# A Strassen level for a weight product, four differences on GpSimd, and two moves in the order of the work

## The chip, the cores and the metric

The kernel runs on one core of a Trainium2 chip. A core has a matrix engine (TensorE, PE in the profile), a vector engine (VectorE, DVE), an activation engine (ScalarE, ACT), a general engine (GpSimd, POOL), a queue engine that issues transfers (SyncE, SP), and DMA engines that move data. Each engine works through its own list of instructions in order and waits on semaphores for the others. The metric is the time of one execution on the device in microseconds (us). Before the change it is 325.35 us (median of 3 runs, 325.21 to 325.37).

## The reference

Inputs are q, k, v of shape (8 batches, 8 heads, 1024 positions, 64), E and F of shape (64, 1024), and weights w1, w2 (512 x 1024) and w_out (1024 x 512). Attention is over a projected sequence of length 64, and its output is the input of a maxout layer:

```python
k_proj = einsum('ks,bhsd->bhkd', E, k)
v_proj = einsum('ks,bhsd->bhkd', F, v)
attn   = softmax(q @ k_proj^T / sqrt(64))          # over the 64 projected positions
x      = (attn @ v_proj) as (8192 tokens, 512)
g      = maximum(x @ w1, x @ w2)
out    = g @ w_out                                 # (8192, 512), float32
```

## The kernel before, in words

The kernel writes the maximum as `x @ w2 + relu(x @ (w1 - w2))`. So `out = x @ M + relu(x @ wd) @ w_out` with `M = w2 @ w_out` (512 x 512) and `wd = w1 - w2`. It makes `wd_sb` on VectorE (`step_wd`, L430), `w2` transposed on TensorE (`step_w2t`, L436) and `m_sb`, which is M, on TensorE (`step_m`, L450) once, near the start, and then goes over the batches.

**Tiles.** A batch has 1024 tokens. The work after attention is cut into 16 units of 512 tokens, two to a batch: unit 0 and 1 are batch 0, unit 2 and 3 are batch 1, and so on. A unit has an "up" half (x @ wd and the relu, `up_steps`, L552) and a "down" half (the sum with M and w_out, `down_steps`, L623). Batch 0's up half is done plainly (`up_slots`, L407, eight blocks for each half of the batch); all other halves are one level of Strassen: a 2 x 2 block product with seven block products instead of eight. The seven are called p1, p2, p6, p5, p7, p3, p4 and come in this order. They share two PSUM banks in turn (X, Y, X, Z, X, Z, X, where Z is Y's bank again). After each product the bank is copied to SBUF by `keep` (L540, tile `p_sb`), or added to what was kept and written to its goal by VectorE. The next product in that bank cannot start before this.

**Sums and differences.** Strassen needs sums of blocks of the left factor and differences of blocks of the right one. `step_s` (L524, instructions on L532) makes the first: `sums_x` of x, `sums_g` of g. `sub4` (L480, instructions on L488) makes the second: `step_t(0)` from w_out, `step_t(1)` from M (both into `T_sb`, for the down half) and `step_tw` from wd (four tiles of 128 x 1024 fp16 in `big0`, used by the up halves from unit 2 on). All of these run on VectorE. In `sub4` the second difference reads the first and the fourth reads the second.

**The order of the work is written by hand.** The pool is in manual schedule, so each engine's list follows the order of the program. `slots` is a list of TensorE steps with keys: `(0, n)` for the start (n = 10 to 15 are batch 0's last up blocks and n = 16 to 19 the four row blocks of M), `("P", n, p, i)` for piece i of product p of unit n's down half, `("U", n, h, i)` for a product of the up half of unit n + 1, and `("G", n, h)` for a group of attention. `at_slot(key, step)` hangs other steps behind a slot. Unit 0's down half has 14 pieces of six matmuls; between them the attention of batch 1 is placed by a list of names (L850 to L871): `kv` (projection of k and v, L188, whose end frees a buffer and lets the loads of batch 2's v and q be issued), `kpt` and `qt` (transposes), `sc` (scores), `dn` and `in` (denominators), `at` (values). From unit 1 on, the attention of the next batch is done in groups (`step_group`, L346) between the pieces.

**Queues.** Loads of q, k, v and of the weights convert float32 to fp16 and are issued by GpSimd. Stores of the result are issued by SyncE, as are the transposing DMAs that make q^T (`step_qt_dma`, L257) from batch 2 on, in two halves of four heads. One queue is one list: a DMA that waits holds back those behind it. Batch 2's q^T is used by the group `("G", 1, 1)` (first half) and `("G", 2, 0)` (second half). The result tiles `o_sb` come from `opool` with 4 buffers. A copy of one element on GpSimd (`step_gate`, L237, tile `junk`) waits for q^T so that later loads do not start earlier.

Of the kernel before, what the change touches and what calls it, by code (L numbers as in the profile page):

```python
# [9 lines left out]
FP16 = mybir.dt.float16  # L10
LN_EXP_SET = 6
ACTF = mybir.ActivationFunctionType
ALU = mybir.AluOpType
# [3 lines left out]
def kernel(  # L17
# [12 lines left out]
    nc = tc.nc  # L30

    B, H, S, D = q.shape
# [5 lines left out]
    NFB = DF // 128  # L38
    NDC = DM // 128
    NP2 = H // 2  # L40
    HALF = S // 2
# [8 lines left out]
    stage = ctx.enter_context(tc.tile_pool(name="stage", bufs=4))  # L50
    xpool = ctx.enter_context(tc.tile_pool(name="xpool", bufs=2))
    gpool = ctx.enter_context(tc.tile_pool(name="gpool", bufs=2))
    opool = ctx.enter_context(tc.tile_pool(name="opool", bufs=4))
    ppool = ctx.enter_context(tc.tile_pool(name="ppool", bufs=4))
    ps = ctx.enter_context(tc.tile_pool(name="ps", bufs=1, space=bass.MemoryType.PSUM))

# [1 line left out]
    turn = [0, 1, 2, 3]  # L58

    def mm_bank(dtype=FP32, n=None):  # L60
        if n is None:
            n = turn.pop(0)
            turn.append(n)
        return ps.tile([128, 512 if dtype == FP32 else 1024], dtype, tag=f"mm{n}", name="mm_ps")

    def att_banks(dtype=FP32):
# [9 lines left out]
            name=nc.get_next_instruction_name(),  # L76
# [82 lines left out]
    for i in range(2):  # L159
        eft_ps = mm_bank()  # L160
        for c in range(NC):
            nc.tensor.transpose(
                out=eft_ps[:, c * KP : (c + 1) * KP],
                in_=ef_v[:, i, c, :],
# [3 lines left out]
        eng = nc.scalar.copy if i else nc.vector.tensor_copy  # L168
# [97 lines left out]
    Z = D // 2  # L266
# [135 lines left out]
    wd_sb = const.tile([128, NDC, DF], FP16)  # L402
    m_sb = const.tile([128, NDC, DM], FP16)
    w2t_sb = big(3).rearrange("p (f m) -> p f m", f=NFB)
# [42 lines left out]
            out=w2t_sb[:, fb : fb + 2, :].rearrange("q f m -> q (f m)"), in_=ps_t  # L447
        )

    def step_m(r):  # L450
        m_ps = mm_bank(n=(1, 2, 0, 3)[r])
        for fb in range(NFB):
            nc.tensor.matmul(  # L453
                out=m_ps, lhsT=w2t_sb[:, fb, r * 128 : (r + 1) * 128], rhs=wo_sb[:, fb, :],
                start=(fb == 0), stop=(fb == NFB - 1),
            )
        nc.scalar.copy(out=m_sb[:, r, :], in_=m_ps)

# [6 lines left out]
    NG = NFB // 2  # L465
    NX = NDC // 2
    CH = DM // 2
    units = [(b, o) for b in range(B) for o in range(2)]
    U = {(b, o): {"n": n, "b": b, "o": o, "t": tiles[b]} for n, (b, o) in enumerate(units)}

    T_sb = const.tile([128, 4, NG + NX, CH], FP16)


    box = {}
# [2 lines left out]
        for i in which:  # L477
            box[i] = big(i)

    def sub4(T, blk, which=range(4)):  # L480
        for i in which:
            out_, x, y = (
                (T[0], blk(0, 1), blk(0, 0)),
                (T[1], blk(1, 1), T[0]),
                (T[2], blk(1, 1), blk(0, 1)),
                (T[3], blk(1, 0), T[1]),
            )[i]
            nc.vector.tensor_tensor(out=out_, in0=x, in1=y, op=ALU.subtract)  # L488

    def step_t(part, which=range(4)):  # L490
        n0, n1, src = ((0, NG, wo_sb), (NG, NG + NX, m_sb))[part]
        hs = n1 - n0
        sub4(
            [T_sb[:, i, n0:n1, :] for i in range(4)],
            lambda h, c: src[:, h * hs : (h + 1) * hs, c * CH : (c + 1) * CH], which,
        )

    def s_g(i):
        return box[2].rearrange("q (s n m) -> q s n m", s=4, n=NG)[:, i]
# [9 lines left out]
    def step_tw(i):  # L509
        sub4(  # L510
            [t_w(i) for i in range(4)],
            lambda h, c: wd_sb[:, h * NX : (h + 1) * NX, c * HALF : (c + 1) * HALF], (i,),
        )

    def x_blk(u, j, h):
# [5 lines left out]
        return u["gt"][:, h * NG : (h + 1) * NG, j * W : (j + 1) * W]  # L521


    def step_s(u, blk, S, which):  # L524
        for i in which:
            x, y, op = (
                (blk(u, 1, 0), blk(u, 1, 1), ALU.add),
                (S(0), blk(u, 0, 0), ALU.subtract),
                (blk(u, 0, 0), blk(u, 1, 0), ALU.subtract),
                (blk(u, 0, 1), S(1), ALU.subtract),  # L530
            )[i]
            nc.vector.tensor_tensor(out=S(i), in0=x, in1=y, op=op)  # L532

    def sums_x(u, which):
        step_s(u, x_blk, lambda i: s_x(i, u), which)
# [197 lines left out]
    t = tiles[0]  # L733
# [35 lines left out]
    u0, u1 = [*up_slots(t, 0)], [*up_slots(t, 1)]  # L769
# [12 lines left out]
    def loads(b, *names):  # L782
# [20 lines left out]
        (None, wd[2]), (None, wt[1]), (6, u1[2]), (7, u1[3]), (None, wt[2]), (None, wt[3]), (8, u0[4]), (9, u0[5]), (None, wd[3]),  # L803
        (10, u1[4]), (11, u1[5]), (12, u0[6]), (13, u0[7]),
        (14, u1[6]), (15, u1[7]),
        *((16 + n, lambda n=n: step_m(n)) for n in range(NDC)),
    ]
    slots = [((0, n), x) for n, x in slots]

# [24 lines left out]
    def at_slot(key, s, *a):  # L834
        steps.setdefault(key, []).append(lambda: s(*a))


    for key, s_, *a in (
        (10, open_box, 1), (11, sums_x, U[0, 0], (2,)), (12, sums_x, U[0, 0], (0,)),
        (13, sums_x, U[0, 0], (1,)), (14, sums_x, U[0, 0], (3,)), (15, open_box, 0, 2),  # L840
        (15, sums_g, U[0, 0], (0, 1)), (16, step_t, 0), (16, sums_g, U[0, 0], (2, 3)),
        *((17 + i // 3, step_tw, i) for i in range(4)), (19, open_box, 3),
    ):
        at_slot((0, key), s_, *a)


    t = tiles[1]
    at_slot((0, 19), new_attn, t)
    at_slot((0, 19), lambda: turn.__setitem__(slice(None), [2, 3]))
    for n, x in enumerate((  # L850
        "", "", "kv", "", "kpt", "qt00 qt10", "", "sc00 sc10", "qt01", "qt11", "",
        "dn00 in00 dn10 in10", "", "", "at00 AT10 sc01",
    )):
        key = ("P", 0, (n - 1) // 2, (n - 1) % 2) if n else (0, 19)
        for name in x.split():
            if name[0] == "k":
                if name == "kpt":
                    at_slot(key, step_kpt, t, 0, H, True)
                else:
                    at_slot(key, step_kv, t, 0, H, "kv", True)  # L860
                    at_slot(key, loads, 2, "v", "q")
            else:
                g, j = int(name[2]), int(name[3])
                s_ = {"qt": step_qt, "sc": step_sc,
                      "dn": step_dn, "in": step_inv, "at": step_at, "AT": step_at}[name[:2]]
                args = (4 * g, 4, 2 * j, 2 * j + 2) if name[:2] == "qt" else (g, j)
                at_slot(key, s_, t, *args, *([True] if name[:2] == "AT" else []))
        if n in (1, 5):
            at_slot(key, step_t, 1, (0, 1) if n == 1 else (2, 3))
        if 6 <= n < 10:  # L870
            at_slot(key, sums_x, U[0, 1], ((2, 0, 1, 3)[n - 6],))  # L871
# [11 lines left out]
    for b in range(3, B):  # L883
        t = tiles[b]
        n = 2 * b - 3
# [74 lines left out]
```

The softmax here doesn't subtract the row's maximum and nothing guards it: scores larger than these inputs give would overflow.

## Time and profile before

| | before |
|---|---|
| time, median of 3 runs | 325.35 us (325.21 to 325.37) |
| span of the profiled execution | 324.9 us, TensorE clock 1.00 |
| TensorE matmul busy | 316.1 us, 97% |
| VectorE busy | 236.6 us, 73%, 420 instructions |
| ScalarE busy | 203.2 us, 63% |
| GpSimd busy | 40.4 us, 12%, 60 instructions |
| moved by DMA | 53.14 MB, 164 GB/s on average |

Busy time is the time in which an engine had an instruction in work. For TensorE the ends are modelled, so a share of 97% says that it rarely stood idle, not that it was at its peak. A group of instructions is shown with its line, engine, operation, output and inputs, count, busy time and the mean duration of one, and then how long the engine stood idle before it and who ended that wait. In a timeline a line is: start, duration, engine, line, operation, with the idle time before in brackets. The window of interest here is the first 90 us, where all that the diff touches lies.

### The profile page before, as it was taken

Reading aid. Unit: us, or ns where it says so; the run is one execution under the profiler, and the core shown is the slowest. Engines: PE = TensorE matmul, PEld = TensorE weight load, DVE = VectorE, ACT = ScalarE, POOL = GpSimd, SP = SyncE. Lnnn points to the kernel's source line nnn. Section 1 sums busy time; section 2 is a strip of 40 time slices with the busy share of each in tenths; the row PEclk is TensorE's granted clock in tenths of the full one; section 3 lists DMA queues with packets and bytes.
Section 4 is the critical chain, followed back from the end, with each engine's and each line's share of the span. In section 5 each row is a group of like instructions: output and inputs, shape, how many; then the busy total and the mean of one; then the engine's idle time right before and its main releaser. Section 6 shows DMA issues by size and latency. Waiting matters only on the chain.

```text
span 324.9 us, 9012 instructions
## 1 busy us (share of the span) xinstructions
PE 316.1 (97%) x3852; PEld 248.5 (76%) x3852; DVE 236.6 (73%) x420; ACT 203.2 (63%) x364; POOL 40.4 (12%) x60
## 2 busy tenths in 40 slices
PE   7989999999999999999999999999999999999995
PEld 3555457877887888878887888868887888888884
DVE  1365797895968787877967786986967796969572
ACT  2366522566776777667776777656776777764541
POOL 8559002003000300021000300030000000000000
PEclk9999999999999999999999999999999999999999
DMA  7999999999999899599969899489959230312133
GB/s 154 206 199 184 205 204 206 217 205 177 204 232 224 140 195 245 149 168 165 228 131 196 152 208 235 131 163 185 228 113 215 51 100 32 99 34 98 34 119 109
DMA packets 76280, 53.14 MB, mean 164 GB/s; under 512 B 29520, under 2 KB 76112, under 8 KB 76240
## 3 DMA queue, kind: packets, MB, share of 16 engines
q0 software_dynamic: 30976, 28.31, 55.3%
q1 hardware_dynamic: 45264, 24.25, 31.2%
q8 instruction: 30, 0.49, 0.6%
q14 instruction: 10, 0.08, 0.1%
HBM read 57.15 MB, written 16.78 MB: 228 GB/s over the span
## 4 chain that ended last, share of the span: by engine, by line
PE 89%; DMA 5%; DVE 4%; issue 1%; POOL 0%; ACT 0%; DVEq 0%; POOLq 0%
PE mm_ps L649 44%; PE mm_ps L571 25%; PE mm_ps L415 4%; PE att_ps L188 4%; PE att_ps L287 3%; PE mm_ps L275 3%; PE mm_ps L453 2%; DMA qt_sb<-q_sb 2%; DMA k_sb<-in_k_dram 2%; DMA kpt_sb<-kp_sb 1%; PE mm_ps L148 1%; PE mm_ps L188 1%; PE mm_ps L246 1%; DVE gt_sb L586 1%; DVE qt_sb L251 1%
## 5 line engine op out<-in xcount | busy, mean ns | idle before, releaser
L542 ACT COPY p_sb<-mm_ps 128x512 f32<-128x512 f32 x172 | 97.2, 594 | 42.1 <-PE mm_ps L571 29.8
L649 PEld LDWEIGHTS <-big 128*128 128x128 f16 x768 | 73.5, 98 | 12.0 <-issue 3.5
L649 PE MATMUL mm_ps<-T_sb,big 128*128 128x256 f16 x576 | 77.9, 273 | 0.0
L586 DVE TENSOR_TENSOR gt_sb<-mm_ps,p_sb 128x512 f16<-128x512 f32 x56 | 38.5, 687 | 47.4 <-PE mm_ps L571 42.7
L571 PE MATMUL mm_ps<-big,big 128*128 128x256 f16 x336 | 50.4, 273 | 0.0
L571 PEld LDWEIGHTS <-big 128*128 128x128 f16 x448 | 43.8, 98 | 5.2
L649 PEld LDWEIGHTS <-gt_sb 128*128 128x128 f16 x384 | 35.8, 98 | 9.9 <-issue 5.4
L649 PE MATMUL mm_ps<-wo_sb,gt_sb 128*128 128x256 f16 x256 | 43.0, 273 | 0.1
L571 PEld LDWEIGHTS <-wd_sb 128*128 128x128 f16 x336 | 32.9, 98 | 3.8
L364 ACT ACTIVATE ex_sb<-mm_ps 128x512 f16<-128x512 f32 x50 | 27.2, 596 | 11.7 <-PE att_ps L287 7.8
L571 PE MATMUL mm_ps<-xt_sb,wd_sb 128*128 128x256 f16 x224 | 33.6, 273 | 0.0
L390 DVE TENSOR_TENSOR xt_sb<-att_ps,ld_sb 128x1024 f16<-128x1024 f32 x26 | 31.7, 1218 | 0.1
L673 DVE TENSOR_TENSOR o_sb<-mm_ps,p_sb 128x512 f32<-128x512 f32 x32 | 21.9, 684 | 7.7 <-PE mm_ps L649 7.7
L649 PE MATMUL mm_ps<-m_sb,xt_sb 128*128 128x256 f16 x128 | 24.4, 273 | 0.0
L238 POOL COPY junk<-qt_sb 1x1 f16<-1x1 f16 x6 | 1.6, 265 | 182.3 <-DMA qt_sb<-q_sb 182.3
L621 ACT ACTIVATE gt_sb<-mm_ps 128x512 f16<-128x512 f32 x28 | 16.8, 600 | 8.7 <-PE mm_ps L571 8.7
L532 DVE TENSOR_TENSOR big<-gt_sb 128x1024 f16<-128x1024 f16 x32 | 21.9, 684 | 0.2
L589 DVE TENSOR_SCALAR gt_sb<-gt_sb 128x512 f16<-128x512 f16 (+1 forms) x56 | 20.4, 365 | 1.9
L649 PE MATMUL mm_ps<-wo_sb,big 128*128 128x256 f16 x128 | 21.5, 273 | 0.0
L649 PE MATMUL mm_ps<-T_sb,gt_sb 128*128 128x256 f16 x128 | 21.5, 273 | 0.0
L649 PEld LDWEIGHTS <-xt_sb 128*128 128x128 f16 x192 | 18.8, 98 | 2.2
L586 DVE TENSOR_TENSOR gt_sb<-p_sb 128x512 f16<-128x512 f32 x28 | 19.1, 680 | 0.0
(87 smaller groups left out, 427.4 us busy)
## 6 DMA issues: line engine op xcount, KB each, us to landing
out_dram<-o_sb SPq DMA_DIRECT2D x63, 256.0 KB, 2.7
k_sb<-in_k_dram POOLq DMA_DIRECT2D x7, 1024.0 KB, 10.8
v_sb<-in_v_dram POOLq DMA_DIRECT2D x7, 1024.0 KB, 17.0
q_sb<-in_q_dram POOLq DMA_DIRECT2D x5, 1024.0 KB, 22.4
q_sb<-in_q_dram POOLq DMA_DIRECT2D x4, 512.0 KB, 21.2
big<-in_moe_w_dram POOLq DMA_DIRECT2D x12, 128.0 KB, 8.2
k_sb<-in_k_dram POOLq DMA_DIRECT2D x4, 256.0 KB, 6.7
q_sb<-in_q_dram POOLq DMA_DIRECT2D x4, 256.0 KB, 7.8
```

Source lines behind the costliest of these rows:

```text
L188: nc.tensor.matmul(out=kv_ps[r * KP : (r + 1) * KP, 0:n], lhsT=eft[:, i, c, :], rhs=t[w][:, h0:h1, c, :], start=(c == 0), stop=(c == NC - 1),)
L364: nc.scalar.activation(out=t["ex", g, j][:, e, :], in_=banks[e], func=ACTF.Exp, scale=scale)
L390: nc.vector.tensor_tensor(out=x_out(t, g, j).rearrange("q z o n -> q o z n"), in0=at_ps.rearrange("q o (z n) -> q o z n", z=2), in1=ld[:, ...
L415: nc.tensor.matmul(out=h_ps, lhsT=wd_sb[:, r, fb * 128 : (fb + 1) * 128], rhs=t["xt"][:, r, :, j * W : (j + 1) * W], start=(r == 0), stop= ...
L532: nc.vector.tensor_tensor(out=S(i), in0=x, in1=y, op=op)
L542: copy(out=x, in_=bank)
L571: nc.tensor.matmul(out=bank[:, m * W : (m + 1) * W], lhsT=w_[:, n_, (2 * d + m) * 128 : (2 * d + m + 1) * 128], rhs=a[:, n_, :], start=(n ...
L586: nc.vector.tensor_tensor(out=c_blk(j, c), in0=two(x), in1=two(y), op=ALU.add)
L589: nc.vector.tensor_scalar_max(ap, ap, 0.0)
L621: nc.scalar.activation(out=out, in_=in_, func=ACTF.Relu)
L649: nc.tensor.matmul(out=bank[:, i * CH : (i + 1) * CH], lhsT=a(c)[:, i * 128 : (i + 1) * 128], rhs=w_(c), start=(n is not None and m == (lo ...
L673: nc.vector.tensor_tensor(out=o_sb, in0=two(x), in1=two(y), op=ALU.add)
```

## The change

Four parts:

1. **M by one Strassen level.** `step_m` (four row blocks, eight matmuls of 512 columns each) becomes `m_steps` with the seven products p1, p2, p6, p5, p7, p3, p4 of eight matmuls of 256 columns each, in slots (0, 16) to (0, 22), in banks 1 and 2. It needs four sums of blocks of w2 transposed (`sums_m`, VectorE, 128 x 1024 fp16, behind slots 11 to 14), the differences of w_out before it instead of during it (`step_t(0)` behind slot 15), and combines its products with four copies on ScalarE, three additions on VectorE and one more copy on ScalarE, where four copies on ScalarE stood before. It is for fewer multiplications on TensorE.
2. **`step_tw` on GpSimd.** The four differences of wd go from VectorE to GpSimd, and `sums_g` and `sums_x` of unit 0 move from slots 11 to 16 to slots 17 to 20. It is for room on VectorE.
3. **Batch 1's attention one piece later.** The list of names gets one empty entry in front, so that its last entry lands in unit 1's first piece, and the groups, the sums of x for unit 2 and the interleaving of unit 1 move by one or two pieces with it.
4. **Batch 2's first q^T half ahead of unit 0's stores.** `step_qt_dma` for heads 0 to 3 moves from `("G", 1, 0)` to `("P", 0, 1, 0)`, in SyncE's list ahead of unit 0's four stores, which wait behind it. It is for an earlier q^T. `opool` gets 7 buffers, so that result tiles can wait.

```diff
-    opool = ctx.enter_context(tc.tile_pool(name="opool", bufs=4))
+    opool = ctx.enter_context(tc.tile_pool(name="opool", bufs=7))
...
-    def step_m(r):
-        m_ps = mm_bank(n=(1, 2, 0, 3)[r])
-        for fb in range(NFB):
-            nc.tensor.matmul(
-                out=m_ps, lhsT=w2t_sb[:, fb, r * 128 : (r + 1) * 128], rhs=wo_sb[:, fb, :],
-                start=(fb == 0), stop=(fb == NFB - 1),
-            )
-        nc.scalar.copy(out=m_sb[:, r, :], in_=m_ps)
...
+            for i in range(2):
+                for c in range(NG):
+                    nc.tensor.matmul(
+                        out=bank[:, i * CH : (i + 1) * CH],
+                        lhsT=a[:, c, i * 128 : (i + 1) * 128],
+                        rhs=w_[:, c, :],
+                        start=(n is not None and i == 0 and c == 0),
+                        stop=(c == NG - 1), skip_group_check=True,
+                    )
...
+        def p1():
+            st["s1"] = keep("pu", product(1, "X", 1))
+        def p2():
+            add(0, 0, product(2, "Y", 2), st["s1"])
+        def p6():
+            st["u1"] = keep("pu", product(6, "X", None))
+        def p5():
+            st["s5"] = keep("pu", product(5, "Z", 2))
+        def p7():
+            st["u2"] = keep("pu", product(7, "X", None))
+        def p3():
+            add(0, 1, product(3, "Z", None), st["u1"])
+            add(1, 1, st["u2"], st["s5"])
+        def p4():
+            nc.scalar.copy(out=block(1, 0), in_=two(product(4, "X", None)))
...
-            lambda h, c: wd_sb[:, h * NX : (h + 1) * NX, c * HALF : (c + 1) * HALF], (i,),
+            lambda h, c: wd_sb[:, h * NX : (h + 1) * NX, c * HALF : (c + 1) * HALF], (i,), nc.gpsimd,
...
-        *((16 + n, lambda n=n: step_m(n)) for n in range(NDC)),
+        *((16 + n, lambda n=n: box["m"][n]()) for n in range(7)),
...
-        for h, (x, y) in enumerate(((5, 1), (1, 2)) if n == 1 else ((2, 2), (2, 3))):
+        for h, (x, y) in enumerate(((6, 1), (0, 2)) if n == 1 else ((2, 2), (2, 3))):
...
-        (10, open_box, 1), (11, sums_x, U[0, 0], (2,)), (12, sums_x, U[0, 0], (0,)),
-        (13, sums_x, U[0, 0], (1,)), (14, sums_x, U[0, 0], (3,)), (15, open_box, 0, 2),
-        (15, sums_g, U[0, 0], (0, 1)), (16, step_t, 0), (16, sums_g, U[0, 0], (2, 3)),
-        *((17 + i // 3, step_tw, i) for i in range(4)), (19, open_box, 3),
+        *((11 + i, sums_m, i) for i in range(4)), (15, step_t, 0), (15, open_box, 0, 1, 2),
+        *((15, step_tw, i) for i in range(4)),
+        (17, sums_g, U[0, 0], (0, 1)), (18, sums_x, U[0, 0], (0, 1)), (19, sums_x, U[0, 0], (2, 3)),
+        (20, sums_g, U[0, 0], (2, 3)), (22, open_box, 3),
...
-        "", "", "kv", "", "kpt", "qt00 qt10", "", "sc00 sc10", "qt01", "qt11", "",
+        "", "", "", "kv", "", "kpt", "qt00 qt10", "", "sc00 sc10", "qt01", "qt11", "",
         "dn00 in00 dn10 in10", "", "", "at00 AT10 sc01",
...
-    at_slot(("P", 0, 6, 0), new_attn, t)
+    at_slot(("P", 0, 1, 0), new_attn, t)
+    at_slot(("P", 0, 1, 0), step_qt_dma, t, 0, H // 2)
...
-    at_slot(("G", 1, 0), step_qt_dma, t, 0, H // 2)
     at_slot(("G", 1, 0), step_qt_dma, t, H // 2, H)
...
-            where = (("P", 1, 0, 2), 0), (("P", 1, 1, 0), 1), (("P", 1, 1, 1), 2), (("U", 1, 0, 1), 3)
+            where = (("P", 1, 1, 0), 0), (("P", 1, 1, 1), 1), (("P", 1, 1, 2), 2), (("U", 1, 0, 1), 3)
```

More of the change, by code (lines that the diff above doesn't have):

```diff
@@ L478, in open_box, with sub4 @@
             box[i] = big(i)
-    def sub4(T, blk, which=range(4)):
+    def sub4(T, blk, which=range(4), eng=nc.vector):
         for i in which:
@@ L487, in sub4 @@
             )[i]
-            nc.vector.tensor_tensor(out=out_, in0=x, in1=y, op=ALU.subtract)
+            eng.tensor_tensor(out=out_, in0=x, in1=y, op=ALU.subtract)
     def step_t(part, which=range(4)):
@@ L496, in step_t, with m_blk, sums_m, m_steps @@
         )
+    def m_blk(j, h):
+        return w2t_sb[:, h * NG : (h + 1) * NG, j * CH : (j + 1) * CH]
+    m_sums = {}
+    def sums_m(i):
+        m_sums[i] = ppool.tile([128, NG, CH], FP16, tag="pd", bufs=4, name="p_sb")
+        sum_s(lambda j, h: m_blk(j, h), lambda n: m_sums[n], i)
+    def m_steps():
+        st = {}
+        two = lambda ap: ap.rearrange("q (i m) -> q i m", i=2)
+        def product(k, name, n):
+            if n is not None:
+                st[name] = mm_bank(n=n)
+            bank = st[name]
+            Bb = lambda h, c: wo_sb[:, h * NG : (h + 1) * NG, c * CH : (c + 1) * CH]
+            T = lambda i: T_sb[:, i, 0:NG, :]
+            a, w_ = {
+                1: lambda: (m_blk(0, 0), Bb(0, 0)), 2: lambda: (m_blk(0, 1), Bb(1, 0)),
+                3: lambda: (m_sums[3], Bb(1, 1)), 4: lambda: (m_blk(1, 1), T(3)),
+                5: lambda: (m_sums[0], T(0)), 6: lambda: (m_sums[1], T(1)),
+                7: lambda: (m_sums[2], T(2)),
+            }[k]()
+            for i in range(2):
[7 more added lines that the diff above has]
+                    )
+            return bank
+        def block(j, c):
+            return m_sb[:, 2 * j : 2 * j + 2, c * CH : (c + 1) * CH]
+        def add(j, c, x, y):
+            nc.vector.tensor_tensor(out=block(j, c), in0=two(x), in1=two(y), op=ALU.add)
+        def p1():
[13 more added lines that the diff above has]
+            nc.scalar.copy(out=block(1, 0), in_=two(product(4, "X", None)))
+        return [p1, p2, p6, p5, p7, p3, p4]
     def s_g(i):
@@ L521, in g_blk, with sum_s @@
         return u["gt"][:, h * NG : (h + 1) * NG, j * W : (j + 1) * W]
+    def sum_s(blk, S, i):
+        x, y, op = (
+            (blk(1, 0), lambda: blk(1, 1), ALU.add),
+            (None, lambda: blk(0, 0), ALU.subtract),
+            (blk(0, 0), lambda: blk(1, 0), ALU.subtract),
+            (blk(0, 1), lambda: S(1), ALU.subtract),
+        )[i]
+        nc.vector.tensor_tensor(out=S(i), in0=S(0) if x is None else x, in1=y(), op=op)
     def step_s(u, blk, S, which):
         for i in which:
[L526 to L532, printed above, removed]
+            sum_s(lambda j, h: blk(u, j, h), S, i)
     def sums_x(u, which):
@@ L835, in at_slot @@
         steps.setdefault(key, []).append(lambda: s(*a))
+    box["m"] = m_steps()
     for key, s_, *a in (
-        (10, open_box, 1), (11, sums_x, U[0, 0], (2,)), (12, sums_x, U[0, 0], (0,)),
-        (13, sums_x, U[0, 0], (1,)), (14, sums_x, U[0, 0], (3,)), (15, open_box, 0, 2),
-        (15, sums_g, U[0, 0], (0, 1)), (16, step_t, 0), (16, sums_g, U[0, 0], (2, 3)),
-        *((17 + i // 3, step_tw, i) for i in range(4)), (19, open_box, 3),
+        *((11 + i, sums_m, i) for i in range(4)), (15, step_t, 0), (15, open_box, 0, 1, 2),
+        *((15, step_tw, i) for i in range(4)),
+        (17, sums_g, U[0, 0], (0, 1)), (18, sums_x, U[0, 0], (0, 1)), (19, sums_x, U[0, 0], (2, 3)),
+        (20, sums_g, U[0, 0], (2, 3)), (22, open_box, 3),
     ):
@@ L847 @@
     t = tiles[1]
-    at_slot((0, 19), new_attn, t)
-    at_slot((0, 19), lambda: turn.__setitem__(slice(None), [2, 3]))
+    at_slot((0, 22), new_attn, t)
+    at_slot((0, 22), lambda: turn.__setitem__(slice(None), [2, 3]))
     for n, x in enumerate((
-        "", "", "kv", "", "kpt", "qt00 qt10", "", "sc00 sc10", "qt01", "qt11", "",
+        "", "", "", "kv", "", "kpt", "qt00 qt10", "", "sc00 sc10", "qt01", "qt11", "",
         "dn00 in00 dn10 in10", "", "", "at00 AT10 sc01",
     )):
-        key = ("P", 0, (n - 1) // 2, (n - 1) % 2) if n else (0, 19)
+        key = ("P", n // 15, (n - 1) // 2 % 7, (n - 1) % 2) if n else (0, 22)
         for name in x.split():
@@ L867 @@
                 at_slot(key, s_, t, *args, *([True] if name[:2] == "AT" else []))
-        if n in (1, 5):
+        if n in (1, 6):
             at_slot(key, step_t, 1, (0, 1) if n == 1 else (2, 3))
-        if 6 <= n < 10:
-            at_slot(key, sums_x, U[0, 1], ((2, 0, 1, 3)[n - 6],))
+        if 7 <= n < 11:
+            at_slot(key, sums_x, U[0, 1], ((2, 0, 1, 3)[n - 7],))
     t = tiles[2]
-    at_slot(("P", 0, 6, 0), new_attn, t)
+    at_slot(("P", 0, 1, 0), new_attn, t)
+    at_slot(("P", 0, 1, 0), step_qt_dma, t, 0, H // 2)
     at_slot(("U", 1, 0, 1), step_kv, t, 0, H, "kv", True)
     at_slot(("U", 1, 0, 4), step_kpt, t, 0, H, True)
-    at_slot(("G", 1, 0), step_qt_dma, t, 0, H // 2)
     at_slot(("G", 1, 0), step_qt_dma, t, H // 2, H)
```

## The prediction, made before the result was known

> **What bounds the kernel now.** I read the page's busy shares first, then the chain of work that ended last in order of time, then the table of stretches around the places that the diff touches, then the timeline of each engine there.
>
> ```profile
> PE 316.1 (97%) x3852; PEld 248.5 (76%) x3852; DVE 236.6 (73%) x420; ACT 203.2 (63%) x364; POOL 40.4 (12%) x60
> ```
>
> ```profile
> 39.86 6.91 PE mm_ps L453 x32
> 46.77 1.31 PE mm_ps L649 x12
> ...
> 69.09 6.50 DMA qt_sb<-q_sb
> ```
>
> ```profile
> 40.00:46.70 6.70, 6.70 (x33) 3.04 (x32) 6.60 (x12) 2.25 (x4) 0.00 (x0) 1.00 1.25 206
> 46.70:64.00 17.30, 17.30 (x261) 13.50 (x260) 13.71 (x28) 7.16 (x11) 2.38 (x3) 1.00 1.30 210
> 64.00:76.00 12.00, 11.20 (x179) 7.94 (x178) 10.18 (x19) 6.76 (x13) 0.18 (x1) 1.00 1.17 213
> ```
>
> TensorE sets the end, so a matmul taken out is worth its full pitch as long as no wait comes in its place. The chain prices it: M's 32 matmuls of 512 columns take 6.91 us (0.216 each), unit 0's 256-column ones 1.31 us for 12 (0.109 each). In the stretches (columns: window, length, busy PE, PEld, DVE, ACT, POOL with counts) TensorE loses time in one alone, 0.80 us between 64 and 76, the wait for batch 2's q^T. The line for 40 to 46.7 is the one to remember: while M is computed, VectorE is busy 6.60 of 6.70 us. It has no room, and nobody waits for it yet.
>
> ```profile
> 37.31 0.69 DVE L426 TENSOR_SCALAR gt_sb<-mm_ps 128x512 f16<-128x512 f32 x1 [0.84 <-PE mm_ps L415]
> ...
> 40.97 0.68 DVE L488 TENSOR_TENSOR T_sb<-wo_sb 128x1024 f16<-128x1024 f16 x1
> 41.69 0.69 DVE L488 TENSOR_TENSOR T_sb<-wo_sb,T_sb 128x1024 f16<-128x1024 f16 x1
> 42.30 0.68 DVE L488 TENSOR_TENSOR T_sb<-wo_sb 128x1024 f16<-128x1024 f16 x1
> ```
>
> VectorE's own pitch: a 128x1024 fp16 sum starts 0.61 us after the one before, 0.72 where it reads that one's result.
>
> **What the Trainium skill says.** "SBUF — State Buffer", section Who interferes with whom: VectorE and GpSimd share a pair of SBUF ports, and a VectorE instruction with two SBUF inputs and a GpSimd instruction that reads SBUF exclude one another for the whole instruction, whichever starts first. The trace has one GpSimd instruction that reads SBUF, the one-element gate, and it agrees in one direction:
>
> ```profile
> 216.25 0.18 POOL L238 COPY junk<-qt_sb 1x1 f16<-1x1 f16 x1 [32.52 <-DMA qt_sb<-q_sb]
> 252.49 0.58 POOL L238 COPY junk<-qt_sb 1x1 f16<-1x1 f16 x1 [33.11 <-DMA qt_sb<-q_sb]
> ```
>
> ```profile
> 252.34 0.69 DVE L532 TENSOR_TENSOR big<-gt_sb 128x1024 f16<-128x1024 f16 x1
> ```
>
> The gate takes 0.18 us, but 0.58 where it starts inside a VectorE sum: that ends at 253.03, the gate at 253.07. For the other direction there is only a hint:
>
> ```profile
> 51.19 1.51 POOL L102 DMA_DIRECT2D q_sb<-in_q_dram  x2
> 51.58 0.48 DVE L209 COPY vp_sb<-vp_sb 64x512 f16<-64x512 f16 x1
> ```
>
> This copy takes 0.29 elsewhere and 0.48 while GpSimd issues loads. "GPSIMD Engine Reference", section Elementwise — side-by-side cycle accounting, prices a two-input sum of 2048 fp32 elements per partition on GpSimd at 4497 ns, and a tight loop at 1.8 cycles an element; no run here shows either. "DMA: Bandwidth & Descriptors", section Issuing engines are not separate DMA queues: transfers of all queues interleave on the same 16 DMA engines. That fits the table, where they are over nine tenths busy at 206 to 213 GB/s.
>
> **The change part by part.**
>
> *M's matmuls.* 56 of 256 columns by 0.109 are 6.12 us against 6.91: -0.79. All of it is on the path.
>
> *M's waits on VectorE, GpSimd left aside.* A product lasts 8 x 0.109 = 0.87 us, and the copy or addition that frees its bank has just the next product to hide behind: 0.59 on ScalarE, 0.69 on VectorE. ScalarE is idle enough (2.25 of 6.70 us). VectorE is not. Its list, from the trace's end of wd at 36.0: sum 0 at 36.05; the relu of slot 12 at 37.31; sum 1 at 37.92; the relu of slot 13 at 38.53; sums 2 and 3 at 39.14 and 39.75; the four differences of w_out at 40.36, 41.08, 41.69, 42.30; then p2's addition, 42.90 to 43.59. TensorE: p1 from 39.86, p2 from 40.73 to 41.61; p6 needs the second difference (41.08 + 0.69) and starts at 41.8; p5 takes the bank of p2, whose addition ends at 43.59, though it could start at 42.7. So p5 to p4 run from 43.65 to 47.15, where M ended at 46.77 before. The waits (0.2 and 0.95) eat the 0.79 and leave **+0.4 us**. The sums of x and g queued behind end about 47.7 and the two late additions about 48.9, and the copy of unit 0's p1 about 50.4; TensorE is then in `kv`, which hides them.
>
> *The four differences on GpSimd.* They can start when wd is whole (36.1), and are needed by unit 2's up half after 65 us, so their own length is hidden, also from the loads queued behind them, which wait for `kv` to about 50. What is not hidden is the port. Per operation, from below: 1024 x 1.8 cycles at 1.2 GHz, 1.54 us by the page's best loop; from above: half of 4497 ns, 2.25 us. The page's sum is of 4-byte elements and ours of 2-byte ones, so I take the middle, 1.9 us, 7.6 for four. Between 36 and 50 almost every VectorE instruction has two SBUF inputs (four sums, four differences, eight sums of x and g). The exceptions, beside which GpSimd can run for nothing, are the two relus, p2's and p3's additions (4 x 0.68 = 2.7 us), and VectorE's idle time from 36 to 40 (4.00 - 3.09 = 0.9 us). The rest, 7.6 - 3.6 = 4.0 us, is pushed into VectorE's list (2.6 at 1.54, 5.4 at 2.25). By the order above that list already stands on the path (p6 waits for the second difference, p5 for the addition), so it is **+4.0 us** on TensorE.
>
> *q^T earlier.* The first half waited for its load until 69.09 and landed at 75.6:
>
> ```profile
> 52.82 10.70 SPq L664 DMA_DIRECT2D out_dram<-o_sb  x4
> 69.09 6.48 SPq L258 DMA_TRANSPOSE qt_sb<-q_sb  x2
> ```
>
> Unit 0's four stores, 1.05 MB, now stand behind it and no longer compete with that load: at 206 GB/s about 5 us. It would land near 70.5, before the 74.7 at which TensorE asks for it: **-0.8**. The new wait holds stores back; of unit 1's tiles three fit in the seven buffers, and the fourth is written at 82 us, long after the first store is out. The second half of q^T stands behind these stores: 70.5 + 5 + 4.4 (its landing) is about 80, the group that uses it comes at 83.7, so nothing.
>
> *One piece later.* Mostly order: the same pieces lie between the last values and the group. One thing differs. Between the last up product and group (1, 1) there was one piece and now there is none, and the scores of that group go into the bank which this product's relu on ScalarE frees about 0.85 us after its end (in the trace 73.77 to 74.62), against 0.45 us of attention in between: **+0.3**, taking the bank as the last wait.
>
> *Sum:* +0.4 + 4.0 - 0.8 + 0.3 = +3.9, **329.2 us**. At the ends of GpSimd's price 327.8 and 330.6.
>
> **The rivals.**
>
> 1. *GpSimd yields.* The port blocks GpSimd behind VectorE, as the gate shows, but not VectorE behind GpSimd: +0.4 - 0.8 + 0.3 = -0.1, 325.2, no change. For it: no VectorE sum in the trace is ever longer than 0.69. Against: no GpSimd instruction of length stands beside one. Chance 0.20.
> 2. *It yields and VectorE is in time.* If p2's addition comes early enough (sums start earlier, or the pitch is better), M gains its whole 0.79, q^T its 0.8: 323.8 to 324.4, faster. For it: the wait that I find is under 1 us and rests on twelve starts. Against: the 6.60 of 6.70 us. Chance 0.27.
> 3. *It costs more.* GpSimd and VectorE take turns one by one, so that each sum waits for a whole GpSimd instruction, and TensorE stands for more than 4 us in one piece: all 7.6 to 9 us less what is free, with q^T late as well, 331 to 333. Chance 0.10.
>
> **How the numbers follow.** The forecast has 0.43. Slower by over 0.2% (above 326.0): forecast and rival 3, 0.53. Within: rival 1, 0.20. Faster (below 324.7): rival 2, 0.27. The range leaves out the far end of rival 3 and the best of rival 2: 324.0 to 331.2.
>
> **What would show it.** VectorE sums between 36 and 50 us that last 1.5 to 2.9 us instead of 0.68, or gaps of that size before them, with a GpSimd TENSOR_TENSOR beside each; TensorE idle between p2 and p5 of M; `kv` of batch 1 at 52 us or later, where it was at 48.1; no wait for q^T near 75, q^T's issue near 64, unit 0's stores after it. The forecast is wrong if VectorE's sums keep their 0.68 us, or if GpSimd's four differences take under 1 us each.

## The result, and the profile after

The changed kernel takes 336.98 us (median of 6 runs, 334.80 to 338.17) beside 325.36 us before (6 runs, 325.21 to 327.74): a ratio of 1.0335, 95% interval 1.0289 to 1.0381. It is 3.35% slower, and slower than my range allowed. Here and below medians and ranges are of all runs, while a ratio leaves out the slow ones, more than 1.5% above the fastest of their kernel. The profiled executions took 326.71 us before and 336.52 us after, with spans of 324.9 and 334.7 us, so the two traces have 9.8 us of difference to show. The other 1.8 of the 11.6 us between the medians are in no trace: the profiled execution of before is 1.35 us above its median, that of after 0.46 below.

The busy shares after:

```profile
PE 318.8 (95%) x3876; PEld 252.2 (75%) x3876; DVE 244.2 (73%) x423; ACT 204.0 (61%) x365; POOL 50.7 (15%) x64
```

GpSimd has gained 10.3 us, and TensorE 2.7 us, although its matmuls were to become cheaper. This says that something is long, not where. The chain of work that ended last, in order of time (start, length, what):

```profile
37.86 0.69 DVE gt_sb L426
38.55 1.14 DVE p_sb L589
...
40.29 4.44 DVE p_sb L589 x2
44.74 2.53 DVE T_sb L480
...
48.04 5.98 PE mm_ps L517 x40
```

Before, the chain in this place was TensorE alone, M's 32 matmuls for 6.91 us. Now it goes through VectorE for ten microseconds: the sums of w2 transposed (L589) and the differences of w_out (L480). The table of stretches (window, length, busy PE, PEld, DVE, ACT, POOL with the number of instructions, then TensorE's clock, the DMA share and GB/s):

```profile
40.00:46.70 6.70, 2.16 (x18) 1.56 (x16) 6.70 (x4) 1.37 (x3) 6.70 (x3) 1.00 1.24 207
46.70:56.00 9.30, 7.96 (x60) 6.34 (x62) 9.16 (x18) 2.35 (x4) 0.01 (x1) 0.82 1.36 202
```

In the first stretch VectorE is busy all the time and has only four instructions in work; before it had twelve. TensorE works 2.16 of 6.70 us. So look at the four, and at what GpSimd does beside them. First VectorE's timeline:

```profile
36.48 0.69 DVE L589 TENSOR_TENSOR p_sb<-big 128x1024 f16<-128x1024 f16 x1
...
38.47 1.22 DVE L589 TENSOR_TENSOR p_sb<-p_sb,big 128x1024 f16<-128x1024 f16 x1
...
40.22 2.00 DVE L589 TENSOR_TENSOR p_sb<-big 128x1024 f16<-128x1024 f16 x1
42.14 2.60 DVE L589 TENSOR_TENSOR p_sb<-big,p_sb 128x1024 f16<-128x1024 f16 x1
44.66 2.60 DVE L480 TENSOR_TENSOR T_sb<-wo_sb 128x1024 f16<-128x1024 f16 x1
47.29 0.69 DVE L480 TENSOR_TENSOR T_sb<-wo_sb,T_sb 128x1024 f16<-128x1024 f16 x1
```

And GpSimd's in the same time:

```profile
36.65 2.50 POOL L480 TENSOR_TENSOR big<-wd_sb 128x1024 f16<-128x1024 f16 x1 [3.80 <-DVE wd_sb L431]
39.23 2.45 POOL L480 TENSOR_TENSOR big<-wd_sb,big 128x1024 f16<-128x1024 f16 x1
41.63 2.56 POOL L480 TENSOR_TENSOR big<-wd_sb 128x1024 f16<-128x1024 f16 x1
44.15 2.56 POOL L480 TENSOR_TENSOR big<-wd_sb,big 128x1024 f16<-128x1024 f16 x1
```

These two lists are one story, if the ends are compared (start plus length). GpSimd's instructions end at 39.15, 41.68, 44.19 and 46.71. VectorE's long sums end at 39.69, 42.22, 44.74 and 47.26: 0.54 or 0.55 us after each of them. And counted from VectorE's end before it (37.17, 39.69, 42.22, 44.74), each GpSimd instruction takes 1.98, 1.99, 1.97 and 1.97 us. They take turns: a VectorE sum works 0.55 us, then a GpSimd difference works 1.97 us, then the next sum. So the wait is written inside the instruction that waits, on both engines, and not as idle time before it. No view of waits shows it; only a length does.

TensorE then, in M and behind it:

```profile
40.25 1.91 PE L517 MATMUL mm_ps<-wo_sb,big 128*128 128x256 f16 x16
48.04 4.23 PE L517 MATMUL mm_ps<-T_sb,p_sb 128*128 128x256 f16 x24 [5.88 <-DVE T_sb L480]
...
52.98 1.04 PE L517 MATMUL mm_ps<-T_sb,big 128*128 128x256 f16 x8
```

p1 and p2 run, then p6 waits 5.88 us for the second difference of w_out. From the start of M to the end of its last matmul it is 40.25 to 54.02, 13.77 us. In the timeline of before it is 39.70 to 46.77, 7.07 us:

```profile
39.70 7.07 PE L453 MATMUL mm_ps<-wo_sb,big 128*128 128x512 f16 x32
```

In what follows "M" is always this stretch, read so. M has lost 6.70 us.

TensorE's waits over the whole execution:

```profile
PE mm_ps L517 <- DVE T_sb L480: 5.9, 1, 5.9
PE mm_ps L275 <- DMA kpt_sb<-kp_sb: 2.5, 1, 2.5
...
PE mm_ps L275 <- ACT gt_sb L682: 0.2, 1, 0.2
```

The second is one that I had not listed; the third is the "one piece later" of my sum. The wait for q^T is gone. To see where the loss is made and given back I take the copy by which ScalarE ends a unit (its last product). Units 0, 1, 8 and 9, before and then after:

```profile
61.76 0.57 ACT L720 COPY o_sb<-mm_ps 128x512 f32<-128x512 f32 x1
82.40 0.59 ACT L720 COPY o_sb<-mm_ps 128x512 f32<-128x512 f32 x1 [0.72 <-PE mm_ps L649]
...
206.95 0.59 ACT L720 COPY o_sb<-mm_ps 128x512 f32<-128x512 f32 x1 [0.72 <-PE mm_ps L649]
226.78 0.59 ACT L720 COPY o_sb<-mm_ps 128x512 f32<-128x512 f32 x1 [0.72 <-PE mm_ps L649]
```

```profile
69.62 0.57 ACT L781 COPY o_sb<-mm_ps 128x512 f32<-128x512 f32 x1
89.03 0.59 ACT L781 COPY o_sb<-mm_ps 128x512 f32<-128x512 f32 x1 [0.72 <-PE mm_ps L710]
...
213.40 0.59 ACT L781 COPY o_sb<-mm_ps 128x512 f32<-128x512 f32 x1 [0.72 <-PE mm_ps L710]
236.55 0.59 ACT L781 COPY o_sb<-mm_ps 128x512 f32<-128x512 f32 x1 [0.72 <-PE mm_ps L710]
```

The copies are late by 7.86 us at unit 0, by 6.63 at unit 1, by 6.45 at unit 8, and by 9.77 from unit 9 to the end. At unit 0 the copy says too much, because ScalarE has other work in front of it. TensorE's last matmuls of that unit, before and after, are these:

```profile
61.17 0.38 PE L649 MATMUL mm_ps<-T_sb,xt_sb 128*128 128x256 f16 x2
```

```profile
68.37 0.38 PE L710 MATMUL mm_ps<-T_sb,xt_sb 128*128 128x256 f16 x2
```

So TensorE is 7.20 us late there, and gets 0.57 back up to unit 1: the q^T wait of 0.80 is gone, and the one of 0.23 is new. There are two losses: one in M, and one of 3.3 us between units 8 and 9. About 0.55 of the 7.20 was there before M: the last VectorE instruction that makes wd starts at 35.33 before and at 35.88 after, and from kernel to kernel it moved between 35.3 and 36.9, also where the program up to there was the same.

### The profile page after: what moved, and what is told of

It is laid out like the page before. It is cut to its first block, busy times and chain, and to the rows that moved or that the text cites. A ratio compares the mean times of both kernels' runs of the same rounds, so it can differ in the third digit from the quotient of the medians.

```text
span 334.7 us, 9073 instructions
## 1 busy us (share of the span) xinstructions
PE 318.8 (95%) x3876; PEld 252.2 (75%) x3876; DVE 244.2 (73%) x423; ACT 204.0 (61%) x365; POOL 50.7 (15%) x64
## 4 chain that ended last, share of the span: by engine, by line
PE 88%; DVE 6%; DMA 4%; issue 1%; POOL 0%; ACT 0%; DVEq 0%; POOLq 0%
PE mm_ps L710 44%; PE mm_ps L632 25%; PE att_ps L188 4%; PE mm_ps L415 3%; PE att_ps L287 3%; PE mm_ps L275 3%; DMA k_sb<-in_k_dram 2%; PE mm_ps L517 2%; DMA kpt_sb<-kp_sb 2%; DVE p_sb L589 2%; DVE T_sb L480 1%; PE mm_ps L148 1%; PE mm_ps L188 1%; PE mm_ps L246 1%; DVE qt_sb L251 1%
## 5 line engine op out<-in xcount | busy, mean ns | idle before, releaser
L603 ACT COPY p_sb<-mm_ps 128x512 f32<-128x512 f32 x176 | 99.7, 593 | 51.8 <-PE mm_ps L632 30.7
L710 PE MATMUL mm_ps<-T_sb,big 128*128 128x256 f16 x576 | 79.0, 275 | 0.0
L589 DVE TENSOR_TENSOR big<-gt_sb 128x1024 f16<-128x1024 f16 x32 | 21.9, 685 | 0.2
```

Of the source, the lines that this page charges most:

```text
L589: nc.vector.tensor_tensor(out=S(i), in0=S(0) if x is None else x, in1=y(), op=op)
L710: nc.tensor.matmul(out=bank[:, i * CH : (i + 1) * CH], lhsT=a(c)[:, i * 128 : (i + 1) * 128], rhs=w_(c), start=(n is not None and m == (lo ...
```

## The experiments

**Theories at the start.** PORT: GpSimd's differences hold VectorE back for their whole length, and part 1 has put VectorE's list on TensorE's path, so that each microsecond counts. Rivals: VectorE's list is too long with or without GpSimd (LIST); the lower clock after TensorE's gap costs the time (CLOCK); the Strassen form itself or the later attention costs something that these waits don't show. Each run has its name in its heading. The kernel before, timed beside them, took 325.83 us (27 runs) for tw_dve_same, tw_dve_late, before_tw_pool and warm_gap; 325.75 (34 runs) for no_strassen, room_on_vector, gate_kpt_after and gate_kpt_before; and 326.0 (35 runs) for two_on_gpsimd, qt_ahead_only and room_gate.

### The four differences back on VectorE, at the same place (tw_dve_same)

```diff
-            lambda h, c: wd_sb[...], (i,), nc.gpsimd,
+            lambda h, c: wd_sb[...], (i,),
```

> The changed kernel with one edit: the four differences of wd run on VectorE, in the same slot 15, instead of on GpSimd. Theory PORT (GpSimd's four instructions of 2.5 us hold the shared SBUF port and make VectorE's sums wait in turn): the sums fall back to 0.68 us; the list before p2's addition grows by 4 x 0.61 = 2.5 us of these differences, so p5 waits about 3.4 us and M ends about 3 us later than before the change; with no late q^T that is 326.5 to 328.5 us. Theory QUEUE (VectorE's list is simply too long for M in seven products, and GpSimd only stood beside it): more work on VectorE, so no better than the changed kernel, 336 us or more.

Measured: 332.0 us (4 runs, 331.91 to 335.19), 1.0214 [1.0178, 1.0250]. GpSimd is out of it, and 5 us of the loss went. The largest part of the rest is VectorE's queue, as the list of waits says:

```profile
PE mm_ps L517 <- DVE m_sb L530: 3.3, 1, 3.3
PE mm_ps L275 <- DMA kpt_sb<-kp_sb: 1.7, 1, 1.7
```

p2's addition, which frees the bank for p5, now stands behind the four differences of wd. The wait of 3.3 us was expected (3.4). The total came out higher than 328.5 because the 32 matmuls behind that wait take 5.3 us, where they take 3.7 in the next run (TensorE's clock reads 0.82 from 46.7 to 56 us here), and because of the wait for `kpt_sb`.

### The four differences on VectorE, behind unit 0's pieces (tw_dve_late)

The edit of the run above, and `step_tw` in new places:

```diff
-        *((15, step_tw, i) for i in range(4)),
...
+    for i, (p, h) in enumerate(((1, 1), (3, 0), (5, 0), (6, 0))):
+        at_slot(("P", 0, p, h), step_tw, i)
```

> The changed kernel with the four differences of wd on VectorE, one by one behind four pieces of unit 0 (products p2, p5... at about 50 to 62 us), where VectorE has idle time. PORT: all of the loss goes; what stays is a wait of about 1 us for p2's addition in M, against 0.8 us of matmuls saved and 0.8 us of q^T wait gone: 324.4 to 325.6 us. QUEUE: the list in front of p2's addition is the same as in the changed kernel, so the loss stays, over 330 us.

Measured: 329.85 us (6 runs, 327.77 to 332.69), 1.0119 [1.0086, 1.0152]. In M this is the kernel that I had worked out "GpSimd left aside":

```profile
42.38 1.05 PE L517 MATMUL mm_ps<-T_sb,p_sb 128*128 128x256 f16 x8 [0.18 <-DVE T_sb L480]
44.18 1.91 PE L517 MATMUL mm_ps<-T_sb,p_sb 128*128 128x256 f16 x16 [0.75 <-DVE m_sb L530]
```

p6 waits 0.18 us for the second difference and p5, the first of the 16 matmuls of the second line, 0.75 for p2's addition; every VectorE sum is back at 0.68. M is 40.29 to 47.83, 7.54 us, 0.47 more than before. Against after's 13.77, the four instructions on GpSimd cost M 6.23 us. But the whole is still 4 us slower than before, and my expectation missed that. The differences have only moved on:

```profile
55.00:71.00 16.00, 14.67 (x250) 10.98 (x249) 15.94 (x32) 8.97 (x14) 0.00 (x0) 1.00 1.20 192
```

From 55 to 71 VectorE is busy 15.94 of 16 us, and TensorE stands 1.33 of them (it stood none before), waiting for copies of q^T and for banks. Then comes 1.7 us for `kpt_sb`. PORT holds for M; LIST is true as well, for smaller amounts.

### The differences on GpSimd in the kernel before (before_tw_pool)

The kernel before with one edit: `step_tw` gets `nc.gpsimd`.

> The kernel before with part 2's engine alone: the four differences of wd on GpSimd, M, the slots and q^T as they were. PORT: VectorE's sums of x and g last up to 2.6 us while GpSimd works, VectorE's list ends near 52 us instead of 48, and the copy of unit 0's p1 comes about 1 us late for TensorE: 326 to 328 us. QUEUE: VectorE has 2.5 us less to do and nobody waits for it: 325.3 us or a little faster.

Measured: 325.75 us (20 runs, 324.91 to 329.50), 1.0003 [0.9988, 1.0018]: no change. Its VectorE is held back just the same:

```profile
39.83 1.74 DVE L532 TENSOR_TENSOR big<-big,xt_sb 128x512 f16<-128x512 f16 x1
41.60 2.23 DVE L532 TENSOR_TENSOR big<-xt_sb,big 128x512 f16<-128x512 f16 x1
43.75 2.60 DVE L532 TENSOR_TENSOR big<-gt_sb 128x1024 f16<-128x1024 f16 x1
```

But M as four plain row blocks takes nothing from VectorE, its TensorE has no wait in the whole region, and VectorE catches up before unit 0 asks. I had expected 326 to 328. So the hold is real, and alone it costs nothing that 20 runs can show; it needs part 1, which puts the held engine on the path. Counted as above, from the end of VectorE's instruction before, GpSimd's four differences take 1.99, 1.97, 1.97 and 1.97 us here, as in after.

### Extra matmuls in TensorE's gap (warm_gap)

```diff
-        (17, sums_g, U[0, 0], (0, 1)), ...
+        (17, warm, 25, True), (17, sums_g, U[0, 0], (0, 1)), ...
```

The changed kernel with 25 matmuls of ones behind p2; nothing reads what they compute.

> The changed kernel with 25 extra matmuls of ones (5.4 us, result unused) behind p2 of M, in the gap in which TensorE waits for VectorE. If part of the loss is a lower TensorE clock after the gap (granted clock 0.82 between 46.7 and 56 us, five products of M at almost twice their time), the clock stays at 1.0 there and about 1.6 us come back, 334 to 336 us. If the clock is not part of it, the time stays or grows by what of the 5.4 us does not fit.

Measured: 337.95 us (4 runs, 335.62 to 338.52), 1.0359 [1.0329, 1.0390]. Its clock reads 1.00 from 46.7 to 56, where after's reads 0.82, and yet unit 0's copy is 7.95 us late, much as in after (7.86). But in this execution M also begins 0.61 us later than in after (40.86 beside 40.25). M itself takes 13.26 us, 0.51 less than in after:

```profile
40.86 1.91 PE L517 MATMUL mm_ps<-wo_sb,big 128*128 128x256 f16 x16
...
53.08 1.04 PE L517 MATMUL mm_ps<-T_sb,big 128*128 128x256 f16 x8
```

M there waits 0.5 us for `T_sb` and 0.75 for `m_sb` behind the extra matmuls: VectorE's list sets the end, and a faster TensorE mostly waits again. The five products behind the gap take 5.46 us with these waits, where after's take 5.98 with none, so as a whole they were not near twice their time. CLOCK is worth about 0.5 of the 6.7 us that M lost. The whole is no faster; its profile has a wait of 3.8 us for `kpt_sb`, where after's has 2.5.

### Part 1 taken back, the rest kept (no_strassen)

`step_m` and the lists of the kernel before, with the differences on GpSimd, batch 1's attention one piece later, and q^T ahead of the stores.

> The changed kernel with part 1 undone: M by step_m, the sums of unit 0 in their old slots; the differences of wd on GpSimd, attention one piece later, q^T ahead of the stores and seven buffers stay. Theory PATH (GpSimd's hold of the port costs only what stands on VectorE's list in front of TensorE, and part 1 is what put it there): VectorE's sums still last up to 2.6 us beside GpSimd, yet nothing waits, and the q^T wait is gone: 324.0 to 325.8 us. Theory PORT ALONE (the hold costs wherever it falls) or a fault of parts 3 and 4: 328 us or more.

Measured: 327.07 us (13 runs, 325.92 to 332.32), 1.0063 [1.0037, 1.0090]. About ten of the 11.6 us are gone with part 1, though VectorE's sums still last up to 2.61 us. Its largest new TensorE wait inside the region is this one:

```profile
PE mm_ps L649 <- DVE p_sb L542: 0.4, 1, 0.4
```

The remaining 0.6% is above what I expected of it. The 0.4 us wait may be part, and so may the 0.2 us for the bank that after has too (`gt_sb`). The rest I could not place, since its profile also starts this region late (wd's last instruction at 36.88; at the very start TensorE waits 0.4 us for the load of F).

### Two of the four differences on GpSimd (two_on_gpsimd)

```diff
-            lambda h, c: wd_sb[...], (i,), nc.gpsimd,
+            lambda h, c: wd_sb[...], (i,), nc.gpsimd if i < 2 else nc.vector,
...
-        *((15, step_tw, i) for i in range(4)),
+        *((15, step_tw, i) for i in range(2)),
...
+    for i, (p, h) in enumerate(((5, 0), (6, 0))):
+        at_slot(("P", 0, p, h), step_tw, 2 + i)
```

> The changed kernel with two of wd's four differences on GpSimd at the same slot and the other two on VectorE behind unit 0's pieces 5 and 6. TURN (each GpSimd instruction holds the port for its whole length, 2.5 us, and VectorE gets one instruction between two of them): the sums wait for two GpSimd instructions in place of four, the last of wo's differences ends about 5 us earlier, M takes 7.9 to 9.5 us (13.5 with four), the whole 328.0 to 331.0. RIVAL (what counts is only that GpSimd is used at all in M, or the first two instructions do the harm): M 11 us or more, the whole 333 or more.

Measured: 332.96 us (5 runs, 332.77 to 334.38), 1.0222 [1.0195, 1.0249]. VectorE's second and third sum last 1.22 and 2.00 us, as in after, and every sum of that size from 42.00 on, after GpSimd's second instruction ended at 41.52, is at 0.68 or 0.69 again. p6's wait falls from 5.88 to 2.05 us:

```profile
44.06 4.53 PE L517 MATMUL mm_ps<-T_sb,p_sb 128*128 128x256 f16 x24 [2.05 <-DVE T_sb L480]
```

M is 40.11 to 50.34, 10.23 us, between what the two theories had said (up to 9.5, or from 11). With none, two and four differences on GpSimd M is 7.54, 10.23 and 13.77 us, so the harm grows with their number. The size I missed is in this line too: 24 matmuls for 4.53 us, where they take 2.79 in a kernel without a gap. The clock reads 0.81 from 40 to 46.7 there. Here, where VectorE has nearly caught up, the slow clock counts in full, 1.7 us.

### Room on VectorE everywhere (room_on_vector)

The changed kernel with all that VectorE could be spared: the differences of wd as above on VectorE behind unit 0's pieces, unit 0's four kept copies on ScalarE, and half of w_out's differences behind p2's addition.

```diff
-            return keep("pd", bank, *([nc.vector.tensor_copy] if u["n"] == 0 else []))
+            return keep("pd", bank, *[])
...
-        ... (15, step_t, 0), ...
+        ... (15, step_t, 0, (0, 1)), ...
+        (17, step_t, 0, (2, 3)), ...
```

> M by Strassen with room made on VectorE: from the changed kernel, the differences of wd on VectorE behind four pieces of unit 0 (as in the run that had this alone), the four copies of unit 0's products on ScalarE instead of VectorE, and the third and fourth difference of w_out behind p2's addition instead of ahead of it. PATH: p5's wait of 0.75 us in M and the waits of unit 0 for VectorE (2.7 of 16 us between 55 and 71) go, M gives its 0.8 us: 323.8 to 326 us. If VectorE was not what TensorE waited for in unit 0, the time stays near that of the run with late differences, 329 to 330 us.

Measured: 331.08 us (6 runs, 328.87 to 334.91), 1.0154 [1.0109, 1.0198]. M has only the 0.18 us wait, and takes 6.63 us (41.19 to 47.82), 0.44 less than plain. Unit 2 ends 0.38 us later than before although wd's last instruction began 1.48 later than before. So up to there the form does gain. But the whole lies above both ranges that I had given. In the profile the loss comes later, 2.8 us between units 8 and 9:

```profile
PE mm_ps L275 <- DMA kpt_sb<-kp_sb: 2.3, 2, 2.0
```

### The second loss: the gate of the loads reads kpt (gate_kpt_after, gate_kpt_before)

In after's second loss TensorE waits for `kpt_sb` at 227.8. GpSimd's list there:

```profile
221.55 0.29 POOL L238 COPY junk<-qt_sb 1x1 f16<-1x1 f16 x1 [32.00 <-DMA qt_sb<-q_sb]
222.06 0.88 POOL L102 DMA_DIRECT2D k_sb<-in_k_dram  x1 [0.22 <-issue]
```

and SyncE's:

```profile
221.86 1.20 SPq L232 DMA_TRANSPOSE kpt_sb<-kp_sb  x1
```

The gate waits for q^T and then lets the next batch's 1 MB loads go. In this execution q^T lands before `kpt_sb`'s small transposing DMA has even been issued (221.55 against 221.86), so the loads start beside it, and it takes 5.9 us to land, where others of the same run take 2.7. TensorE waits 2.5 us, and its clock reads 0.57 from 228 to 232. From unit 8's copy to unit 9's it is 23.15 us; in gate_kpt_after, without the wait, it is 19.11. So beside the 2.5 us of waiting some 1.5 are lost behind it, where the clock is low.

The order is not peculiar to this execution. In all six profiles of kernels with part 1 and this gate (after, tw_dve_same, tw_dve_late, warm_gap, two_on_gpsimd, room_on_vector) the gate comes 0.27 to 0.32 us ahead of `kpt_sb`'s issue in one batch, and that `kpt_sb` takes 5.1 to 7.2 us. In the four without part 1 (before, before_tw_pool, no_strassen, qt_ahead_only) the gate never comes first. Why part 1 changes the order is not shown. The edit makes the gate of these batches read `kpt` instead:

```diff
+    def step_gate_kpt(t):
+        nc.gpsimd.tensor_copy(out=junk, in_=t["kpt"][0:1, 0, 0:1])
...
-        at_slot(("U", n, 0, 6), step_gate, t)
+        at_slot(("U", n, 0, 6), step_gate_kpt, t)
```

> The changed kernel, with the gate that releases the next batch's loads (batches 3 to 7) reading one element of k projected and transposed (kpt) instead of q^T. Theory RACE: in the changed kernel q^T lands before kpt's transposing DMA is issued, the next batch's loads start within 0.3 us of it and compete with it, kpt lands after 5.9 us instead of 2.7 and TensorE waits 2.5 us at about 225 us, with a lower clock after it. Then here kpt lands in 2.7 to 3 us in every batch, no wait for it is left, and 2.5 to 3.5 us come back: about 333 us. If the late kpt is chance in the memory or comes from something else, a wait of 1 us or more for kpt stays and so does the time, 336 to 338.

Measured: 333.31 us (5 runs, 333.07 to 334.91), 1.0246 [1.0217, 1.0275], 3.7 us below after's median. TensorE waits for `kpt_sb` no more, and it lands in time:

```profile
DMA to landing us min/median/max: 2.7/2.7/3.4
```

The second loss is this race.

The same edit in the kernel before:

> The kernel before with the same gate on kpt. RACE: its wait of 0.8 us for kpt at 219 us goes: 324.3 to 325.3 us. Otherwise no change; if the loads then come too late for a later batch, slower.

Measured: 326.35 us (22 runs, 324.71 to 327.99), 1.0014 [0.9999, 1.0028]. It gains nothing there, where I had expected about 1 us; its profile still shows 1.3 us of wait for `kpt_sb`, with the loads held back until later. What makes `kpt_sb` late in the kernel before is open.

### Part 4 alone (qt_ahead_only)

The kernel before with `opool` at 7 and the first q^T half ahead of unit 0's stores.

> The kernel before with part 4 alone: batch 2's first half of q^T issued ahead of unit 0's stores, and the larger output pool it needs. THEORY: TensorE's wait for q^T (1.0 us in the profile of before) goes and about 0.8 us is saved: 324.7 to 325.2 beside 325.75. RIVAL: that wait is there in only some runs, or is given back at the next transfer (the kpt of a later batch), so 325.4 to 326.2.

Measured: 325.41 us (14 runs, 324.41 to 331.36), 0.9987 [0.9966, 1.0009]. Its profile has neither the q^T wait nor the one for `kpt_sb`, and a span of 322.7 us; over all runs the gain of 0.6 us is not clear of the noise, and the median is the rival's. One run of 331.36 stands out.

### Room on VectorE, and the gate that reads kpt (room_gate, room_gate_again)

Both edits together, the best version that I could put together with part 1 in it.

> The kernel with all of VectorE's list relieved (differences of wd on VectorE behind unit 0's pieces, unit 0's four kept copies on ScalarE, the second half of wo's differences behind p2's addition), and with the gate ahead of the next batch's loads reading kpt instead of q^T. THEORY (the loss is VectorE's list on TensorE's path, plus the late kpt): M stays within 0.3 us of its plain 6.9 us, no wait for kpt, and the whole is 324.0 to 326.0, even with the kernel before (325.75) or a little under. RIVAL (the Strassen products themselves or the later attention cost something that no wait shows): 328 or more without a kpt wait.

Measured: 329.52 us (22 runs, 325.04 to 332.28), 1.0047 [1.0022, 1.0073]. Ten of the 22 runs lie above 330 us and are not in this ratio; by the medians of all runs it is 1.1% longer than the kernel before. The profiled execution took 325.36, with M at 6.63 us and units 2 to 8 ending 0.5 us earlier than before, units 9 to 14 1.3 us earlier, so no cost of the Strassen form that waits don't show is seen in it. But most of its runs were longer than that. A second execution of it:

> The same kernel as room_gate, looked at once more, because its executions spread from 325.0 to 332.3 and the first profile fell on one of the short ones (325.36). CLOCK: if this execution is one of the longer ones (328 or more), the granted clock is below 1.0 somewhere in it, with no TensorE wait longer than in the first profile. TRANSFERS: in a longer execution a wait for a transfer (kpt, q^T, v or k) of 1 us or more is found that the first does not have.

Measured: this execution took 330.4 us. Up to unit 1 it equals the short one within 0.1 us, and then it has this, where the short one has none:

```profile
PE mm_ps L278 <- DMA qt_sb<-q_sb: 3.5, 1, 3.5
```

It is the second half of batch 2's q^T. In the short execution it is issued at 72.50 and lands 10.7 us later, at 83.2, and its first scores run at 83.27: just in time. In the long one it is issued at 73.12, lands 13.5 us later, and the scores start at 86.62. The clock reads 0.91 from 76 to 90. Two profiles show that this transfer decides between these two executions; whether it decides all of the 22 is not shown. No version with part 1 came out ahead of the kernel before in its median.

## Why the prediction was wrong

The direction was right, and so in the main was the mechanism: GpSimd holds VectorE back, and part 1 has put VectorE's list on TensorE's path. The sum was too small: +3.9 us predicted, +11.6 measured in the medians and 9.8 in the two profiles. Two of its terms failed. The differences on GpSimd, put at 4.0 us, cost 6.2. And the later batches, put at nothing, cost 3.3.

- **M's matmuls, -0.79, and M's waits without GpSimd, +0.4.** Right. With the differences elsewhere the two waits are 0.18 and 0.75 us (predicted 0.2 and 0.95), and M is 0.47 us longer than before. With the waits removed it is 0.44 shorter.
- **The differences on GpSimd, +4.0.** This step failed, and hardly in its price. I took 1.9 us for each; their own work is 1.97, four times 7.9. What failed is "The exceptions, beside which GpSimd can run for nothing": I counted 3.6 us as free. VectorE's instructions were stretched by 0.54, 1.32, 1.92 and 1.92 us over their 0.68, together 5.7, so only 2.2 us were free. p2's and p3's additions (half of my 2.7) were no cover: they run at 49.1 and 53.7, and GpSimd is done at 46.71. Without these 1.4 us my 3.6 would have been the 2.2. From 42.2 on GpSimd had only two-input instructions beside it and pushed out its whole length. The other 0.5 of the 6.2 us is the clock, a term that I did not have: behind p6's start M's last 40 matmuls take 5.98 us in after, but 5.45 in tw_dve_late and 5.46 in warm_gap, which wait 0.75 us among them at a clock of 1.00. With the 0.47 above this is the whole of M's 6.7 us. That the two exclude one another for the whole instruction is what the Trainium skill says ("SBUF — State Buffer", Who interferes with whom); the runs agree in both directions, with VectorE's 0.68 us stretched to 2.60 and GpSimd's 1.97 to 2.56. "GPSIMD Engine Reference", section Elementwise — side-by-side cycle accounting, gave me the estimates 1.54 us, from its best loop, which is not a two-input one, and 2.25, from its two-input sum; 1.97 lies between.
- **q^T, -0.8.** Right for its first half: no such wait in after. It landed at 76.5 and not at 70.5, since all before it was 7 us later. "So nothing" for the second half was wrong where TensorE is on time: room_gate's second profile waits 3.5 us for it.
- **One piece later, +0.3.** Measured 0.23. With q^T this is the 0.57 us given back between units 0 and 1.
- **A wait that was in no step.** 3.3 us at `kpt_sb`, more than any other error of the sum. The order of two DMA queues that nothing fixes, `kpt_sb`'s issue and the gate, came out the wrong way. I had looked at the first 90 us only, because the diff ends there, and that is no reason to put the rest at nothing.
- **The rivals.** The third had the mechanism: turns one by one, and TensorE standing for more than 4 us in one piece (5.88). I gave it 0.10, and ended the range at the lower part of it; its late q^T did not come, and its 331 to 333 us are still too few. The first two fall: VectorE does not keep its 0.68.

In order of size: part 1 and part 2 together, 6.2 us, which neither costs alone (part 2 alone 0.0 in before_tw_pool; part 1 without it 0.47 in M); the `kpt_sb` race, 3.3; the start, about 0.5, by chance as far as is known; less what q^T and the later piece give together, about 0.6.

## What to carry to other kernels

Work moved to GpSimd to make room on VectorE made no room here, because both had two-input elementwise instructions at that time: they took turns, and the slower one set the pace. Before counting any of it as free, lay both lists side by side in time and ask which VectorE instruction stands beside each GpSimd instruction and who waits for it. And before a change that puts an engine's results on TensorE's path, ask how full that engine is there (6.60 of 6.70 us here): an engine nobody waits for and one that sets the pace look alike in the busy shares. And look at the whole span: with a change that ends at 90 us, two queues came in another order at 220.

## What the runs showed that I had not expected

- The wait for the other engine's turn is part of the recorded length, 2.60 us for a sum that works 0.55 to 0.68, and up to 2.56 for a GpSimd difference of 1.97. The page's idle times and waits do not show it.
- After waits of 5.88 us (after), 3.29 (tw_dve_same), 2.05 (two_on_gpsimd) and 2.01 (room_on_vector) TensorE's clock falls: in stretches of 2 us it reads 0.50 to 0.56 at its lowest, and within some 5 us of the wait's end it is back at 1.00. After the 2.5 us at 227 it is 0.54. Waits of 1.70 (tw_dve_late) and 1.72 (tw_dve_same) and shorter ones left it at 1.00. So a gap of 2 us or more cost these kernels the gap and, where nothing else was waited for, 1.5 to 1.7 us behind it.
- The small transposing DMA of `kpt_sb` mostly took 2.7 us to land, and 5.1 to 7.2 in the six batches in which the gate had let the next loads start 0.3 us before it; a q^T half took 10.7 or 13.5 us in two executions of one program.
